# Binding the next pair's operands behind the current pair's adds on VectorE and ScalarE, in the last stage of an attention, token-mixing and MLP kernel

## The chip, the cores and the metric

The kernel runs on one core of a Trainium2 chip. The metric is device time in microseconds, the median of the runs shown. A second number, the span of one profiled execution, is what the rows of the trace add up to.

## The reference, cut to what matters

```
kv  = einsum('bhsd,bhse->bhde', k, v);  out = einsum('bhsd,bhde->bhse', q, kv)
x   = out / sqrt(mean(out*out) + 1e-6) * g_norm          # 8 batches of 576 tokens, 512 features
x   = x + y + relu((x + y) @ w_ch)                       # y: token mixing of x*cos, x*sin
u   = x + transpose(relu(xT @ w_tok1) @ w_tok2)
out = u + relu(u @ w_ch1) @ w_ch2                        # 512 -> 1536 -> 512: the last stage
```

The change touches only the last line, the feed-forward block over the 4608 tokens of u.

## The kernel before

All matrix products are done in float16 pairs: a value is split into a high part and a low part (the rest), and each product is three matmuls on TensorE, high by high, high weight by low operand, and low weight by high operand, summed in PSUM (lines 82 to 84, function `mm3`).

The last stage works on pairs of token blocks of 288 columns. There are 8 pairs, 0 to 7. A pair's two halves of features and two blocks of tokens make a 2 by 2 matrix of blocks, and the product with the weights is done with seven block products in place of eight (products 1 to 7, the Winograd form of Strassen's scheme). So each pair needs seven operands, sums and differences of its four blocks.

`chunks(i)` makes the operands of pair i. It is a generator that is advanced in four steps. The first loads the blocks into the tile `c` (u in the code) by four DMAs from the scratch tensor `u2d` and allocates the operand tiles; the other three compute the operands: ScalarE writes the high parts `o0` (seven of them, index 0 to 6), VectorE writes differences into `t` (four of them) and the low parts `o1`, and at the end ScalarE scales `c` in place. The tiles `o0` and `o1` have one buffer each, so they can be written only when the pair before has read its operands for the last time. In the trace both are called `o`, numbers being left out; in listings of the order, `o40` and `o41` are the high and low operands of pair 4.

`mlp(i)` works off pair i. The hidden features come in six groups g of 128. Each group takes seven products of 6 matmuls with the first weights `wa` into the PSUM tiles `pa`, `pb` and `pc` (products 1, 6, 7 and 4 add up in `pa` one after the other, with a read by ScalarE after each; product 2 goes to `pb`, 5 and 3 to `pc`). ScalarE copies the partial sums to `m`, `u` and `own`; VectorE adds `pb` and `pc` to `own`, forms `pre` from the last of `pc`, and four values `sum`. Of these seven hidden operands ScalarE writes the high parts `gh` (three from `own`, four from `sum`) and VectorE the low parts `gl`. For the second weights `wb`, the tiles `na` (m = 0, 1), `nb` and `nc` take products over all six groups, 18 matmuls each: first product 1 into `na` and product 2 into `nb`, which VectorE adds to `c` (function `add`), then products 5, 6, 7, 3 and 4 into `nc` and `na`, each behind an add that has read what lay in that tile. 504 matmuls make a pair.

Names in the order: `na30` is the tile na of pair 3 for m = 0, `gh35` the high hidden operands of pair 3, group 5. "Body" is used below for the groups' work of a pair, "tail" for the second half of products 5, 6, 7, 3 and 4, "head" for the start of the next body.

What sets the order: the program is written in the order above, and a scheduler then orders each engine's instructions by its own estimate of when they are ready, within the dependences and the program's priorities. The generator's steps are called at fixed places in `mlp`: the first after the adds of products 1 and 2, the next two after the adds of product 6 for m = 0 and m = 1, the last after product 3 of m = 0. The scheduler moves them from there. Each engine runs its queue strictly in that order.

Of the kernel before, what the change touches and what calls it, by code (L numbers as in the profile page):

```python
# [13 lines left out]
AF = mybir.ActivationFunctionType  # L14
ALU = mybir.AluOpType
# [5 lines left out]
SW = 32.0  # L21
# [7 lines left out]
def attn_mixer_kernel(  # L29
# [4 lines left out]
    nc = tc.nc  # L34
# [27 lines left out]
    def bank(name):  # L62
        return ps.tile([P, 512], F32, tag="ps", name=name)
# [88 lines left out]
    def words(w):  # L152
        return (w, 1) if w.dtype == F32 else (w.bitcast(I32), 2)
# [91 lines left out]
    def load_heads(b):  # L245
        o = Batch()
        o.b, o.zh = b, None
        o.kv = []
        for r in range(3 if b else NR + 1):
            load_kv(o, r)  # L250
        o.q = fp.tile([P, HP, SM + P], F32, tag="q", name=f"q{b}", bufs=1)
        qs = qT[b].rearrange("h p s -> p h s")
        nc.sync.dma_start(o.q[:, :, :S], qs)

        nc.sync.dma_start(o.q[:, :, S:], qs[:, :, SM:])
        return o
# [247 lines left out]
    def chunks(i):  # L504

        u = (cp[0] if i % 2 else cw).tile([P, KD, 2, NC], F32, tag="c", name=f"c{i}")
        oh, ol = (cw.tile([P, 7, DH, NC], F16, tag=f"o{j}", name=f"o{i}{j}") for j in range(2))
        if i:
            t = cp[0].tile([P, 4, DH, NC], F32, tag="t", name=f"t{i}")
        else:  # L510

            t = zp.tile([P, KM + 1, DM], F16, tag="zh", name="t0").rearrange("p k d -> p (k d)").bitcast(F32)
            t = t[:, :4 * DH * NC].rearrange("p (x k n) -> p x k n", x=4, k=DH)
        for k in (slice(0, DH), slice(DH, KD)):
            for n in range(2):
                at = (2 * i + n) * NC
                nc.sync.dma_start(u[:, k, n, :], u2d[:, k, at:at + NC])
        b11, b12, b21, b22 = u[:, :DH, 0], u[:, :DH, 1], u[:, DH:, 0], u[:, DH:, 1]
        yield u, oh, ol
        for x, src in ((0, b11), (1, b21), (2, b22)):  # L520
            nc.scalar.activation(oh[:, x], src, AF.Copy, scale=1.0 / SW)
        nc.vector.tensor_tensor(t[:, 0], b12, b11, ALU.subtract)
        nc.vector.tensor_tensor(t[:, 1], b22, t[:, 0], ALU.subtract)
        for x, src in ((0, b11), (1, b21)):
            nc.vector.scalar_tensor_tensor(ol[:, x], src, 1.0 / SW, oh[:, x], ALU.mult, ALU.subtract)
        nc.scalar.activation(oh[:, 3:5], t[:, :2], AF.Copy, scale=1.0 / SW)
        yield
        nc.vector.tensor_tensor(t[:, 2], b12, b22, ALU.subtract)
        nc.vector.tensor_tensor(t[:, 3], b21, t[:, 1], ALU.subtract)
        nc.vector.scalar_tensor_tensor(ol[:, 3:5], t[:, :2], 1.0 / SW, oh[:, 3:5], ALU.mult, ALU.subtract)  # L530
        nc.scalar.activation(oh[:, 5:], t[:, 2:], AF.Copy, scale=1.0 / SW)
        yield
        nc.vector.scalar_tensor_tensor(ol[:, 2], b22, 1.0 / SW, oh[:, 2], ALU.mult, ALU.subtract)
        nc.vector.scalar_tensor_tensor(ol[:, 5:], t[:, 2:], 1.0 / SW, oh[:, 5:], ALU.mult, ALU.subtract)
        nc.scalar.activation(u, u, AF.Copy, scale=1.0 / SW)

    def mlp(i, ck, following):

        u, oh, ol = ck
# [6 lines left out]
        def wide(p, g, acc, first):  # L546
            ws, xs = PRODUCTS[p]
            mm3(acc, [(wa[0][:, g, k, ws], wa[1][:, g, k, ws], oh[:, xs, k], ol[:, xs, k]) for k in range(DH)], first, skip_group_check=True)

        def part(name, g):  # L550
            return cp[0].tile([P, NC], F32, tag=name, name=f"{name}{i}{g}", bufs=2)

        def sums_high(h, g):
            nc.scalar.activation(h.hi[:, 3:], h.s, AF.Copy)  # L554
            nc.vector.tensor_tensor(h.lo[:, 3:], h.s, h.hi[:, 3:], ALU.subtract)  # L555


        def step(n, between=lambda: None):
            g = hidden[n] if n < KH else None
            h = hidden[n - 1] if n else None  # L560
            if g:
                g.a = bank(f"pa{i}{n}")[:, :NC]
                wide(1, n, g.a, True)
                m1 = part("m1", n)
                nc.scalar.activation(m1, g.a, AF.Copy)
            if h:
                wide(7, n - 1, h.a, False)
                u3 = part("u3", n - 1)
                nc.scalar.activation(u3, h.a, AF.Copy)
            if n > 1:  # L570
                sums_high(hidden[n - 2], n - 2)
            between()
            if g:
                pb = bank(f"pb{i}{n}")[:, :NC]
                wide(2, n, pb, True)
                g.own = cp[0].tile([P, 3, NC], F32, tag="own", name=f"own{i}{n}", bufs=2)
                nc.vector.tensor_tensor(g.own[:, 0], pb, m1, ALU.add)
            if h:
                h.c = bank(f"pc{i}{n - 1}")[:, :NC]
                wide(5, n - 1, h.c, True)  # L580
                nc.vector.tensor_tensor(h.own[:, 2], h.c, u3, ALU.add)
            between()
            if g:
                wide(6, n, g.a, False)
                g.u2 = part("u2", n)
                nc.scalar.activation(g.u2, g.a, AF.Copy)
            if h:
                wide(4, n - 1, h.a, False)
                nc.scalar.activation(h.own[:, 1], h.a, AF.Relu)
                nc.scalar.activation(h.own[:, 0::2], h.own[:, 0::2], AF.Relu)  # L590
                between()
                wide(3, n - 1, h.c, False)
                h.hi = cp[0].tile([P, 7, NC], F16, tag="gh", name=f"gh{i}{n - 1}", bufs=KH)
                h.lo = cp[0].tile([P, 7, NC], F16, tag="gl", name=f"gl{i}{n - 1}", bufs=KH)
                nc.scalar.activation(h.hi[:, :3], h.own, AF.Copy)
                pre = part("pre", n - 1)
                nc.vector.tensor_tensor(pre, h.c, h.u2, ALU.add)  # L597
                h.s = cp[0].tile([P, 4, NC], F32, tag="sum", name=f"sum{i}{n - 1}", bufs=2)
                nc.vector.scalar_tensor_tensor(h.s[:, 0], pre, 0.0, h.own[:, 0], ALU.max, ALU.subtract)
                nc.vector.scalar_tensor_tensor(h.s[:, 2], pre, 0.0, h.own[:, 2], ALU.max, ALU.subtract)  # L600
                nc.vector.tensor_tensor(h.s[:, 1], h.own[:, 2], h.s[:, 0], ALU.subtract)
                nc.vector.tensor_tensor(h.s[:, 3], h.own[:, 1], h.s[:, 1], ALU.subtract)
                nc.vector.tensor_tensor(h.lo[:, :3], h.own, h.hi[:, :3], ALU.subtract)  # L603

        def narrow(p, m, g, acc, first):
            ws, xs = PRODUCTS[p]
            h = hidden[g]
            part = (wb[0][:, g, m, ws], wb[1][:, g, m, ws], h.hi[:, xs], h.lo[:, xs])
            mm3(acc, [part], first=first and g == 0, last=g == KH - 1, skip_group_check=True)

        def add(acc, m, half, n, last=False):
            ct = half * MH + m
            dst = u[:, ct, n, :]
            nc.vector.scalar_tensor_tensor(dst, acc, 1.0 / SW**2, dst, ALU.mult, ALU.add)  # L614
            if last:
                at = (2 * i + n) * NC
                nc.sync.dma_start(outf[:, ct, at:at + NC], dst)
# [7 lines left out]
        def side(g):  # L625
            for acc, p, name in ((pa, 1, "na"), (pb, 2, "nb")):
                for m in range(MH):
                    if g == 0:
                        acc[m] = bank(f"{name}{i}{m}")[:, :NC]
                    narrow(p, m, g, acc[m], True)  # L630

        step(KH, lambda: side(next(start)))
        for g in start:
            side(g)
# [3 lines left out]
        for m in range(MH):  # L638
            add(pa[m], m, 0, 0)
            add(pb[m], m, 0, 0, True)  # L640
        nxt = next(following, None)

        def run(p, m, acc, first):
            if acc[m] is None:
                acc[m] = bank(f"nc{i}{m}")[:, :NC]
            for g in range(KH):
                narrow(p, m, g, acc[m], first)
# [67 lines left out]
    nxt = load_heads(1)  # L715
# [40 lines left out]
    for b in range(B):  # L756
        loaded.clear()
        if b == 0:
# [10 lines left out]
            src, _ = words(w_tok1)  # L769
# [49 lines left out]
        o, nxt = nxt, after  # L819
# [10 lines left out]
    for i in range(pairs):  # L830
        ck = mlp(i, ck, chunks(i + 1) if i + 1 < pairs else iter(()))
# [40 lines left out]
```

## Time and profile before

| | us |
|---|---|
| median of 3 runs | 1155.57 |
| lowest, highest | 1155.48, 1162.52 |
| the profiled execution's own time | 1159.02 |
| its span | 1157.3 |
| TensorE busy in the span | 1086.3 |
| VectorE, ScalarE busy | 825.4, 560.2 |

The time is that of the whole execution, the span what the profiler records of it; 1.7 us of the profiled execution lie outside its span. The last stage, from the first pair on, begins near 640 us. One thing to know for reading the timelines: a matmul's row shows how long it was under way, while the next one starts some 0.12 us behind it.

### The profile page before, as it was taken

Reading aid. Unit: us, or ns where it says so; the run is one execution under the profiler, and the core shown is the slowest. Engines: PE = TensorE matmul, PEld = TensorE weight load, DVE = VectorE, ACT = ScalarE, POOL = GpSimd, SP = SyncE. Lnnn points to the kernel's source line nnn. Section 1 sums busy time; section 2 is a strip of 40 time slices with the busy share of each in tenths; the row PEclk is TensorE's granted clock in tenths of the full one; section 3 lists DMA queues with packets and bytes.
Section 4 is the critical chain, followed back from the end, with each engine's and each line's share of the span. In section 5 each row is a group of like instructions: output and inputs, shape, how many; then the busy total and the mean of one; then the engine's idle time right before and its main releaser. Section 6 shows DMA issues by size and latency. Waiting matters only on the chain.

```text
span 1157.3 us, 21691 instructions
## 1 busy us (share of the span) xinstructions
PE 1086.3 (94%) x8884; PEld 821.8 (71%) x8884; DVE 825.4 (71%) x1475; ACT 560.2 (48%) x958; POOL 225.7 (20%) x290
## 2 busy tenths in 40 slices
PE   4779988998998999989999999999999999999998
PEld 3566766675875767657677777777777777777776
DVE  4998858777787887868746494848577584848483
ACT  3757526455455454554623373625355362726260
POOL 2351033462642725426100000000000000000000
PEclk9779989998998999989999999999999999999999
DMA  9535564775748738663192801011010202010101
GB/s 323 194 131 103 118 168 112 200 181 130 237 95 209 190 98 216 148 159 90 44 273 56 300 1 57 26 42 42 27 57 12 72 12 73 1 66 18 37 7 42
DMA packets 146084, 126.36 MB, mean 109 GB/s; under 512 B 93184, under 2 KB 121984, under 8 KB 145984
## 3 DMA queue, kind: packets, MB, share of 16 engines
q1 hardware_dynamic: 140608, 104.53, 33.9%
q0 software_dynamic: 5376, 20.45, 5.1%
q8 instruction: 69, 1.13, 0.4%
q14 instruction: 31, 0.25, 0.1%
HBM read 74.29 MB, written 29.88 MB: 90 GB/s over the span
## 4 chain that ended last, share of the span: by engine, by line
PE 37%; DVE 30%; DMA 13%; ACT 9%; POOL 6%; issue 4%; SPq 1%; POOLq 0%; ACTq 0%; DVEq 0%
DMA xt<-xs 3%; PE na L82 3%; PE na L84 3%; PE na L83 3%; DVE gl L555 3%; DVE gl L603 3%; DVE cs L358 3%; DMA c<-u2d 2%; DMA u2d<-R 2%; PE pa L82 2%; ACT gh L554 2%; PE pa L83 2%; PE pa L84 2%; PE nc L84 1%; PE nc L82 1%
## 5 line engine op out<-in xcount | busy, mean ns | idle before, releaser
L82 PE MATMUL py<-wmh,zh 128*128 128x256 f16 (+1 forms) x576 | 165.9, 288 | 4.3 <-ACT zh L361 2.7
L83 PE MATMUL py<-wml,zh 128*128 128x256 f16 (+1 forms) x576 | 165.8, 288 | 0.0
L84 PE MATMUL py<-wmh,zl 128*128 128x320 f16 (+1 forms) x512 | 146.0, 287 | 3.2 <-DVE zl L363 3.2
L82 PE MATMUL na<-gh,wbh 128*128 128x288 f16 x384 | 107.6, 286 | 9.3 <-DVE c L614 9.3
L82 PE MATMUL pa<-o,wah 128*128 128x288 f16 x384 | 108.6, 286 | 1.1 <-DVE pre L597 1.1
L83 PE MATMUL pa<-o,wah 128*128 128x288 f16 x384 | 109.3, 286 | 0.0
L83 PE MATMUL na<-gl,wbh 128*128 128x288 f16 x384 | 109.3, 286 | 0.0
L84 PE MATMUL na<-gh,wbl 128*128 128x288 f16 x384 | 109.2, 286 | 0.0
L84 PE MATMUL pa<-o,wal 128*128 128x288 f16 x384 | 108.6, 286 | 0.0
L82 PE MATMUL pr<-uh,wch 128*128 128x256 f16 (+1 forms) x256 | 77.1, 302 | 11.0 <-ACT uh L419 11.0
L83 PEld LDWEIGHTS <-wbh 128*128 128x128 f16 x672 | 65.7, 98 | 26.8 <-issue 10.4
L555 DVE TENSOR_TENSOR gl<-sum,gh 128x1152 f16<-128x1152 f32 x48 | 65.0, 1354 | 24.3 <-ACT gh L554 23.5
L83 PE MATMUL pr<-ul,wch 128*128 128x256 f16 (+1 forms) x256 | 77.3, 302 | 5.1 <-DVE ul L422 5.1
L83 PEld LDWEIGHTS <-wah 128*128 128x128 f16 x672 | 65.7, 98 | 18.5 <-issue 2.0
L82 PEld LDWEIGHTS <-wah 128*128 128x128 f16 x672 | 65.7, 98 | 16.6
L84 PEld LDWEIGHTS <-wbl 128*128 128x128 f16 x672 | 65.7, 98 | 16.6
L82 PEld LDWEIGHTS <-wbh 128*128 128x128 f16 x672 | 65.7, 98 | 16.6
L84 PEld LDWEIGHTS <-wal 128*128 128x128 f16 x672 | 65.7, 98 | 16.6
L84 PE MATMUL pr<-uh,wcl 128*128 128x256 f16 (+1 forms) x256 | 77.1, 301 | 0.0
L614 DVE SCALAR_TENSOR_TENSOR c<-na,c 128x288 f32<-128x288 f32 x64 | 28.9, 452 | 64.5 <-PE na L84 64.5
L82 PEld LDWEIGHTS <-zh 128*128 128x128 f16 x576 | 56.9, 99 | 21.1 <-ACT zh L361 3.4
L301 POOL TENSOR_TENSOR ri<-ss,mhalf 128x8 f32<-128x8 f32 x40 | 70.2, 1756 | 2.4
(292 smaller groups left out, 2931.4 us busy)
## 6 DMA issues: line engine op xcount, KB each, us to landing
q<-in_q SPq DMA_DIRECT2D x8, 1152.0 KB, 7.1
c<-u2d SPq DMA_DIRECT2D x32, 288.0 KB, 4.3
out<-c SPq DMA_DIRECT2D x64, 144.0 KB, 1.7
k<-in_k SPq DMA_DIRECT2D x24, 256.0 KB, 6.6
v<-in_v SPq DMA_DIRECT2D x24, 256.0 KB, 6.7
wa_r<-in_w_ch SPq DMA_DIRECT2D x24, 256.0 KB, 4.2
wb_r<-in_w_ch SPq DMA_DIRECT2D x24, 256.0 KB, 4.3
wad<-wa POOLq DMA_DIRECT2D x24, 224.0 KB, 3.4
```

The costliest lines, as they stand in the source:

```text
L82: nc.tensor.matmul(acc, ah, bh, start=first and i == 0, stop=False, **more)
L83: nc.tensor.matmul(acc, ah, bl, start=False, stop=False, **more)
L84: nc.tensor.matmul(acc, al, bh, start=False, stop=last and i == n - 1, **more)
L301: nc.gpsimd.tensor_tensor(ri, ss, mhalf, ALU.pow)
L358: nc.vector.tensor_tensor(cs, cs, x.unsqueeze(1).to_broadcast([P, 2, DM]), ALU.mult)
L554: nc.scalar.activation(h.hi[:, 3:], h.s, AF.Copy)
L555: nc.vector.tensor_tensor(h.lo[:, 3:], h.s, h.hi[:, 3:], ALU.subtract)
L603: nc.vector.tensor_tensor(h.lo[:, :3], h.own, h.hi[:, :3], ALU.subtract)
L614: nc.vector.scalar_tensor_tensor(dst, acc, 1.0 / SW**2, dst, ALU.mult, ALU.add)
```

## The change

`keep_in_program_order` puts an edge from an instruction to the one that was written just ahead of it on the same engine: it may not be queued earlier than that one. It makes no instruction wait for another's end. `placed` applies it, for all pairs but the first, to six instructions of the generator: the first high part, the first difference of each of the two difference steps, the high parts 5 and 6, the low part 2 and the scaling of `c`. Instructions between them aren't bound. The generator's first step, with the loads, is now written ahead of the last body step, so that its edges refer to the places where the later steps are called.

```
+        def placed(ins):
+            if i:
+                tc.keep_in_program_order(ins)
         yield u, oh, ol
         for x, src in ((0, b11), (1, b21), (2, b22)):
-            nc.scalar.activation(oh[:, x], src, AF.Copy, scale=1.0 / SW)
-        nc.vector.tensor_tensor(t[:, 0], b12, b11, ALU.subtract)
+            ins = nc.scalar.activation(oh[:, x], src, AF.Copy, scale=1.0 / SW)
+            if x == 0:
+                placed(ins)
+        placed(nc.vector.tensor_tensor(t[:, 0], b12, b11, ALU.subtract))
         nc.vector.tensor_tensor(t[:, 1], b22, t[:, 0], ALU.subtract)
...
-        nc.vector.tensor_tensor(t[:, 2], b12, b22, ALU.subtract)
+        placed(nc.vector.tensor_tensor(t[:, 2], b12, b22, ALU.subtract))
...
-        nc.scalar.activation(oh[:, 5:], t[:, 2:], AF.Copy, scale=1.0 / SW)
-        yield
-        nc.vector.scalar_tensor_tensor(ol[:, 2], b22, 1.0 / SW, oh[:, 2], ALU.mult, ALU.subtract)
+        placed(nc.scalar.activation(oh[:, 5:], t[:, 2:], AF.Copy, scale=1.0 / SW))
+        yield
+        placed(nc.vector.scalar_tensor_tensor(ol[:, 2], b22, 1.0 / SW, oh[:, 2], ALU.mult, ALU.subtract))
         nc.vector.scalar_tensor_tensor(ol[:, 5:], t[:, 2:], 1.0 / SW, oh[:, 5:], ALU.mult, ALU.subtract)
-        nc.scalar.activation(u, u, AF.Copy, scale=1.0 / SW)
+        placed(nc.scalar.activation(u, u, AF.Copy, scale=1.0 / SW))
...
+        nxt = next(following, None)
         step(KH, lambda: side(next(start)))
...
-        nxt = next(following, None)
-
         def run(p, m, acc, first):
```

Up to the last stage no engine's order changes. In it, three places matter.

VectorE, the end of pair 3's body, from the last `pre` to the add of product 1 (line numbers after are 7 higher). Before:

```order
L597 TENSOR_TENSOR pre35_10000<-pc35_9951,u235_9898 128x288
L525 SCALAR_TENSOR_TENSOR o41_10054<-c4_10052,o40_10053 128x576 x2
L599 SCALAR_TENSOR_TENSOR sum35_10002<-pre35_10000,own35_9882 128x288
L600 SCALAR_TENSOR_TENSOR sum35_10002<-pre35_10000,own35_9882 128x288
L533 SCALAR_TENSOR_TENSOR o41_10054<-c4_10052,o40_10053 128x576
L530 SCALAR_TENSOR_TENSOR o41_10054<-t4_10055,o40_10053 128x1152
L601 TENSOR_TENSOR sum35_10002<-own35_9882,sum35_10002 128x288
L614 SCALAR_TENSOR_TENSOR c3_9335<-na30_9935,c3_9335 128x288
```

and now:

```order
L604 TENSOR_TENSOR pre35_10008<-pc35_9959,u235_9898 128x288
L532 SCALAR_TENSOR_TENSOR o41_9927<-c4_9925,o40_9926 128x576
L606 SCALAR_TENSOR_TENSOR sum35_10010<-pre35_10008,own35_9882 128x288
L607 SCALAR_TENSOR_TENSOR sum35_10010<-pre35_10008,own35_9882 128x288
L608 TENSOR_TENSOR sum35_10010<-own35_9882,sum35_10010 128x288
L621 SCALAR_TENSOR_TENSOR c3_9208<-na30_9943,c3_9208 128x288
```

Of the next pair's low parts one (index 1) still stands ahead of the add of `na30`; one more of that size, the low part 2 and the double low part 3 and 4 now stand behind it.

TensorE, the same place: the last matmuls ahead of product 6 into `na30` (the first of which ends each piece). Before, ahead of it stand products 1 and 2 of pair 4's first group (`pa40`, `pb40`):

```order
L83 MATMUL pb40_10282<-o41_10054,wah_6749 128x288
L84 LDWEIGHTS wal_6750
L84 MATMUL pb40_10282<-o40_10053,wal_6750 128x288
L82 LDWEIGHTS wbh_7391
L82 MATMUL na30_9935<-gh30_9638,wbh_7391 128x288
```

and now the last ones of product 2 of pair 3:

```order
L83 MATMUL nb31_9955<-gl35_10006,wbh_7391 128x288
L84 LDWEIGHTS wbl_7392
L84 MATMUL nb31_9955<-gh35_10005,wbl_7392 128x288
L82 LDWEIGHTS wbh_7391
L82 MATMUL na30_9943<-gh30_9638,wbh_7391 128x288
```

Of pair 4's first two groups 52 matmuls were queued within pair 3's tail before; now it is 24, and all of them behind the first matmuls of product 6.

VectorE, the differences `t`. Before, those for pair 5 stood in the body of pair 4:

```order
L577 TENSOR_TENSOR own42_10392<-pb42_10385,m142_10373 128x288
L522 TENSOR_TENSOR t5_10772<-c5_10769 128x576
L555 TENSOR_TENSOR gl40_10356<-sum40_10360,gh40_10355 128x1152
L523 TENSOR_TENSOR t5_10772<-c5_10769,t5_10772 128x576
L528 TENSOR_TENSOR t5_10772<-c5_10769 128x576
L529 TENSOR_TENSOR t5_10772<-c5_10769,t5_10772 128x576
```

and now those for pair 4 stand among the adds of pair 3's tail:

```order
L562 TENSOR_TENSOR gl35_10006<-sum35_10010,gh35_10005 128x1152
L532 SCALAR_TENSOR_TENSOR o41_9927<-c4_9925,o40_9926 128x576
L621 SCALAR_TENSOR_TENSOR c3_9208<-nc30_10060,c3_9208 128x288
L621 SCALAR_TENSOR_TENSOR c3_9208<-na30_9943,c3_9208 128x288
L529 TENSOR_TENSOR t4_9928<-c4_9925 128x576
L621 SCALAR_TENSOR_TENSOR c3_9208<-nc31_10107,c3_9208 128x288
L621 SCALAR_TENSOR_TENSOR c3_9208<-na31_9947,c3_9208 128x288
L535 TENSOR_TENSOR t4_9928<-c4_9925 128x576
L530 TENSOR_TENSOR t4_9928<-c4_9925,t4_9928 128x576
```

The four differences have left the body. The double low parts (indices 3 and 4, then 5 and 6) and low part 2 follow them in the tail, and on ScalarE the high parts 3 to 6 and the scaling of `c`. The DMA queue's order is the same before and after.

## Rows read from the trace of the kernel before

**Rows 1.** The page: busy time, and the granted clock in 40 slices.
```profile
PE 1086.3 (94%) x8884; PEld 821.8 (71%) x8884; DVE 825.4 (71%) x1475; ACT 560.2 (48%) x958; POOL 225.7 (20%) x290
...
PEclk9779989998998999989999999999999999999999
```

**Rows 2.** Busy time by stretches of the last stage, one stretch a pair.
```profile
core 0: us, PE busy (x) PEld busy (x) DVE busy (x) ACT busy (x) POOL busy (x), PEclk, DMA share, GB/s
...
883.80:947.70 63.90, 61.95 (x504) 49.29 (x504) 43.17 (x79) 30.23 (x49) 0.00 (x0) 1.00 0.12 38
...
sum 466.70, PE 452.73 PEld 359.98 DVE 306.87 ACT 210.25 POOL 0.00; mean PE 64.68 PEld 51.43 DVE 43.84 ACT 30.04 POOL 0.00
```

**Rows 3.** Who TensorE waited for, 640 us to the end: total, times, longest.
```profile
PE na L82 <- DVE c L614: 9.3, 6, 1.9
PE pa L82 <- DVE pre L597: 1.1, 2, 0.9
```

**Rows 4.** Timeline of TensorE, pair 3's end: start, length, operation, idle before.
```profile
872.35 0.29 PE L84 MATMUL pa<-o,wal 128*128 128x288 f16 x1
...
881.66 0.29 PE L84 MATMUL pb<-o,wal 128*128 128x288 f16 x1
883.88 0.28 PE L82 MATMUL na<-gh,wbh 128*128 128x288 f16 x1 [1.94 <-DVE c L614]
...
907.28 0.29 PE L84 MATMUL pa<-o,wal 128*128 128x288 f16 x1
```

**Rows 5.** Timeline of VectorE, the same stretch.
```profile
876.39 1.36 DVE L555 TENSOR_TENSOR gl<-sum,gh 128x1152 f16<-128x1152 f32 x1 [1.74 <-ACT gh L554]
877.67 1.05 DVE L603 TENSOR_TENSOR gl<-own,gh 128x864 f16<-128x864 f32 x1
878.64 0.45 DVE L597 TENSOR_TENSOR pre<-pc,u 128x288 f32<-128x288 f32 x1
879.00 1.41 DVE L525 SCALAR_TENSOR_TENSOR o<-c,o 128x576 f16<-128x576 f32 x2
880.34 0.45 DVE L599 SCALAR_TENSOR_TENSOR sum<-pre,own 128x288 f32<-128x288 f32 x1
880.71 0.45 DVE L600 SCALAR_TENSOR_TENSOR sum<-pre,own 128x288 f32<-128x288 f32 x1
881.08 0.75 DVE L533 SCALAR_TENSOR_TENSOR o<-c,o 128x576 f16<-128x576 f32 x1
881.75 1.35 DVE L530 SCALAR_TENSOR_TENSOR o<-t,o 128x1152 f16<-128x1152 f32 x1
883.01 0.45 DVE L601 TENSOR_TENSOR sum<-own,sum 128x288 f32<-128x288 f32 x1
883.38 0.45 DVE L614 SCALAR_TENSOR_TENSOR c<-na,c 128x288 f32<-128x288 f32 x1
```

**Rows 6.** Timeline of ScalarE, the same stretch.
```profile
874.33 0.68 ACT L590 ACTIVATE own<-own 128x576 f32<-128x576 f32 x1 [3.10 <-DVE own L581]
874.91 0.39 ACT L589 ACTIVATE own<-pa 128x288 f32<-128x288 f32 x1
875.21 1.15 ACT L554 ACTIVATE gh<-sum 128x1152 f16<-128x1152 f32 x1
...
907.60 0.41 ACT L589 ACTIVATE own<-pa 128x288 f32<-128x288 f32 x1 [13.12 <-PE pa L84]
```

**Rows 7.** Timeline of VectorE in the body of pair 4.
```profile
913.47 0.76 DVE L522 TENSOR_TENSOR t<-c 128x576 f32<-128x576 f32 x1 [1.19 <-DMA c<-u2d]
...
916.46 0.76 DVE L523 TENSOR_TENSOR t<-c,t 128x576 f32<-128x576 f32 x1 [0.96 <-DMA c<-u2d]
...
923.08 1.36 DVE L555 TENSOR_TENSOR gl<-sum,gh 128x1152 f16<-128x1152 f32 x1 [0.74 <-ACT gh L554]
...
928.96 1.36 DVE L555 TENSOR_TENSOR gl<-sum,gh 128x1152 f16<-128x1152 f32 x1 [0.74 <-ACT gh L554]
```

**Rows 8.** Busy time in the rest of pair 3's tail, columns as in rows 2.
```profile
883.90:907.50 23.60, 23.60 (x193) 18.86 (x193) 9.10 (x19) 3.65 (x8) 0.00 (x0) 1.00 0.13 44
```

## The prediction

> **What bounds the kernel now.** The page comes first: TensorE is busy for 94% of the span, VectorE for 71%, and from the middle of the span on the granted clock is at its full level, 2.4 GHz [rows 1]. So in the last stage time can only be won where TensorE stands still. The table by stretches tells how much that is: over seven stretches from 690.6 us on TensorE is busy for 452.73 of 466.70 us, and a pair's 504 matmuls take 61.95 us, 0.1229 us each [rows 2]; I count 0.1225 where they run without a gap. Some of the missing 14 us lie behind the last matmul and can't be touched. What can be touched stands in the list of waits: 9.3 us in six stops of the first matmul of product 6 into `na`, which waits for an add on VectorE (L614), and 1.1 us in two stops at `pa` [rows 3]. That is 10.4 us, the ceiling of any gain here and 0.9% of the time. There are seven places where one pair passes into the next; the first had no such stop.
>
> The timelines then show how a stop arises, at the end of pair 3. TensorE issues the last matmul of `pb` at 881.66 and the next one, into `na`, at 883.88, after 1.94 us of idling [rows 4]. The add that it waits for starts at 883.38 on VectorE, which has been working without a break since 876.39: two `gl`, a `pre`, and then, between the `sum` of the last group, four steps for the next pair's low parts, L525 twice, L533 and L530 [rows 5]. The chain of ScalarE that starts it begins late, too. The last matmul of the last group's product 4 is issued at 872.35 [rows 4]. ScalarE can read such a result 0.32 us after that matmul's start: 907.28 and 907.60 in a place where it was waiting for it [rows 4, 6]. But here it reads at 874.91, since the step ahead of it (L590) waited for VectorE until 874.33 [rows 6]. It is late by 874.91 - 872.35 - 0.32 = 2.24 us. I call this VectorE's backlog, B.
>
> **The change, part by part.** *The low parts that leave the chain.* One L525 (0.67 us by the step from 881.08 to 881.75 of the like L533), L533 (0.67) and L530 (881.75 to 883.01, 1.26) no longer stand ahead of the add: 2.60 us less [rows 5]. One low part stays there (0.67). The chain from ScalarE's read of product 4 to TensorE's go is now, by starts: read to `gh` 0.30, `gh` to `gl` 1.18 [rows 5, 6], `gl` L555 1.28, `gl` L603 0.97, `pre` 0.36, one low part 0.67, three `sum` 0.37 each, and 0.50 from the add's start to the matmul [rows 4, 5]. The sum is 6.37 us, where it was 883.88 - 874.91 = 8.97. After pairs 0, 2, 4 and 6 a fourth `sum` stands ahead of the add as well, at most 0.45 more.
>
> *The matmuls that leave the cover.* Before, 76 matmuls lay between the end of product 4 and product 6 of `na`; now, with pair 4's first products moved behind, it is 53 after the pairs 1, 3 and 5, 56 after 2, 4 and 6, and 57 after pair 0 (counted in the order). TensorE's own work is the same, so this costs nothing by itself, but it arrives at the add earlier: after 6.49 us in place of 9.31, or after 6.86 and 6.98. The cover loses 2.82 us where the chain loses 2.60. So what is to be won does not hang on the low parts but on B. With 0.20 us from the end of product 4's issue to the read (0.32 less a matmul's 0.12), the stop is 0.20 + B + 6.37 - 6.49 = 0.08 + B after an odd pair, and at most 0.20 + B + 6.82 - 6.86 = 0.16 + B after an even one.
>
> *The backlog.* The trace does not show B in the new order, so I bound it. Its upper end is today's 2.24. Its lower end is zero, and a reckoning of VectorE's body work leads there. From one `gl` L555 to the next in the crowded part of the body it is 5.88 us, of which 0.74 waiting for `gh`: 5.14 us of work for a group [rows 7]. In the new order VectorE has to do, between the first `pre` of the body and the fourth `sum` of group 4, five groups' work less one `gl` (1.28) and less two `own` adds (0.4 each): 25.7 - 2.1 = 23.6 us, and with two waits of 0.74 us 25.1. The first `pre` can begin when product 3 of group 0 is through, 72 matmuls into the body, at 8.8 + 0.2 = 9.0 us; the fourth `sum` then ends at 34.1. Product 4 of group 5 ends 279 matmuls into the body after an odd pair, 274 after an even one, at 34.2 or 33.6; ScalarE has read it 0.5 us later, at 34.7 or 34.1. So the sum is there when ScalarE comes to it, and B is between 0 and 0.3. What has left the body to make this so: four differences `t` of some 0.67 us each and two waits for the load of `c`, 1.19 and 0.96 us [rows 7], together 4.8 us. What has come into it is group 0's work, which before began in the tail ahead. I take a stop of 0.2 us at each of the seven places, nearer to the lower end, since the reckoning ends there: 1.4 us.
>
> One thing in this sum is a matter of how rows are read. A VectorE step of 0.45 us is followed by the next one 0.37 us after its start [rows 5], so I count starts, not lengths. The Trainium skill ("VectorE: DVE Perf Modes", "The DRAIN you can't avoid") says that the next operation does not start until the pipeline is empty; counted by full lengths the chain would be 0.57 us longer, and seven times that would put the time at an estimated 1150.6. The row shows an overlap of 0.08 us at every one of these steps, and the sum goes by it.
>
> *The two stops at `pa`* (1.1 us) wait for a `pre`, and so for the same backlog; I count them as gone.
>
> *What moved into the tail.* VectorE is busy for 9.10 of 23.60 us there, ScalarE for 3.65 [rows 8]. Four differences, two double and two single low parts (2.7 + 2.5 + 1.3 = 6.5 us) and on ScalarE some 5 us of high parts and scaling fit in. TensorE's work hides them, and the nearest due time is that of the second L532, low part 0: it stands behind four adds, a `sum`, `gh` (1.18) and `gl` (1.28) and is done 4.4 us after the add of `na30` starts, while TensorE needs it 54 matmuls after it starts product 6, at 0.5 + 6.6 = 7.1 us. The cover is 2.7 us. All later operands have more, being due at the next body's first matmuls or after. The early call of the generator's first step moves no load: the DMA queue's order is unchanged.
>
> Sum: 10.4 - 1.4 = 9.0 us won. The profiled execution took 1159.02 us (1157.3 of span and 1.7 outside) and would take 1150.0; that execution was 3.45 us above the median of the runs, and I carry the difference over to the median: 1155.57 - 9.0 = 1146.6 us.
>
> **The rivals.** *Some backlog stays.* The reckoning of B takes VectorE as running without other waits, and 25 us of it leave room for an error of a microsecond. At B = 1 the stops are 1.1 us each, 7.7 in all; the gain is 2.7 and the time 1152.9. For it: the new order has VectorE idle at the head of the body and crowded behind, as now. Against it: the 4.8 us that left the body.
>
> *The backlog stays as it is, and the kernel gets slower.* This is one mechanism at one place: the cover of product 6 shrinks by 2.82 us while the chain shrinks by 2.60. At B = 2.24 each of the seven stops is 2.3 us, 16.2 together in place of 10.4, and the time is 1161.4. It decides from B = 1.4 on, where seven stops of 1.48 us make today's 10.4. For it speaks that today's B of 2.24 comes from the same engine doing the same work; against it, that the reckoning would have to be wrong by 1.4 us at every pair.
>
> *The next pair's operands come late.* If the second L532 is done over 2.7 us later than I work out, TensorE stops there, and from 4.2 us on (2.7 and the 1.5 won at a place) the change loses. Nothing in the tail's rows is near that full [rows 8].
>
> *The change does not do what it says* is ruled out for the adds, which the order shows ahead of three of the four low parts; that one low part stays ahead is in the sum.
>
> **How the numbers follow.** The time is 1155.57 - 10.4 + 7 x stop. I give 0.70 to a backlog under about 0.45 us (1145.2 to 1149), with 1146.6 for its likeliest value; 0.17 to a backlog from there to 1.4 (1149 to 1155.6); 0.08 to more (1161.4 at 2.24); 0.03 to late operands; 0.02 to anything else. The range for 8 in 10 goes from just under the ceiling, 1144.8, to 1153.0, which takes in the first case and most of the second. A change of 1%, 11.6 us, is about what a measurement of this kernel can tell from none. Faster by more than that would take more than all of TensorE's idle time here: 0.04. Slower by more than that needs a backlog over 3.1 us or operands late by some 6 us: 0.04. The rest, 0.92, is within 1%.
>
> **What would show it.** In the new profile the list of waits for TensorE should have `na` on the add at under 0.4 us a time, and the `pa` stops should be gone; a pair should take 61.9 to 62.2 us from product 6 to product 6 in place of 63 to 65. ScalarE's L596 (now L589) should start within 0.6 us of product 4's end, and VectorE should show the `t` and low parts in the tail. The prediction is wrong if that ScalarE step is still 1 us or more late (then the stop is that long), or if TensorE shows stops at `pa` or `pb` behind a low part `o`.

## The result and the profile after

The changed kernel takes 1146.62 us (median of 6 runs, 1144.02 to 1148.35) where the kernel before took 1156.62 (6 runs, 1155.48 to 1162.52) beside it: a ratio of 0.990, 95% interval 0.988 to 0.993. The profiled execution of the changed kernel took 1148.35 us, 1146.6 of it span.

The page of the kernel after, busy time and granted clock, answers to [rows 1]:

```profile
PE 1079.8 (94%) x8884; PEld 819.2 (71%) x8884; DVE 823.6 (72%) x1475; ACT 561.9 (49%) x958; POOL 229.4 (20%) x290
...
PEclk9889998999999999989999999999999999999999
```

TensorE's share looks unchanged, since busy time and span both went down; its busy time fell in the stages ahead of the last one (590.6 us before, 584.8 after) and hardly within it (495.7 and 495.0). The last stage by itself tells more. From the first matmul into `pa` to the end of the span it took 1157.3 - 647.6 = 509.7 us before and 1146.6 - 648.0 = 498.6 after, 11.1 us less; up to it the two profiled executions are within 0.4 us.

Busy time by stretches, one from product 6 to the next product 6, columns as in [rows 2]:

```profile
877.15:939.10 61.95, 61.90 (x505) 49.31 (x504) 43.46 (x79) 31.11 (x49) 0.00 (x0) 1.00 0.12 39
815.32:877.15 61.83, 61.83 (x505) 49.31 (x504) 42.71 (x77) 30.26 (x48) 0.00 (x0) 1.00 0.12 39
```

A pair now takes hardly longer than its matmuls, whose 504 spacings of 0.1225 us make 61.7 us: 61.8 to 62.0 us from product 6 to product 6, where it was 62.8 to 65.1. The list of TensorE's waits from 640 us on, which had eight stops [rows 3], is empty; in the groups by line 0.2 us are left, at the first matmul of product 6:

```profile
L82 PE MATMUL na<-gh,wbh 128*128 128x288 f16 x384 | 106.0, 286 | 0.2
```

The end of pair 3 on TensorE, then on ScalarE, then on VectorE, answers to [rows 4 to 6] (lines 7 higher):

```profile
870.44 0.29 PE L84 MATMUL pa<-o,wal 128*128 128x288 f16 x1
...
876.94 0.29 PE L84 MATMUL nb<-gh,wbl 128*128 128x288 f16 x1
877.15 0.28 PE L82 MATMUL na<-gh,wbh 128*128 128x288 f16 x1
```

```profile
870.77 0.41 ACT L596 ACTIVATE own<-pa 128x288 f32<-128x288 f32 x1
871.07 1.16 ACT L561 ACTIVATE gh<-sum 128x1152 f16<-128x1152 f32 x1
```

```profile
872.26 1.36 DVE L562 TENSOR_TENSOR gl<-sum,gh 128x1152 f16<-128x1152 f32 x1 [1.44 <-ACT gh L561]
873.54 1.05 DVE L610 TENSOR_TENSOR gl<-own,gh 128x864 f16<-128x864 f32 x1
874.50 0.45 DVE L604 TENSOR_TENSOR pre<-pc,u 128x288 f32<-128x288 f32 x1
874.87 0.75 DVE L532 SCALAR_TENSOR_TENSOR o<-c,o 128x576 f16<-128x576 f32 x1
875.54 0.45 DVE L606 SCALAR_TENSOR_TENSOR sum<-pre,own 128x288 f32<-128x288 f32 x1
...
876.64 0.82 DVE L621 SCALAR_TENSOR_TENSOR c<-na,c 128x288 f32<-128x288 f32 x2
...
880.33 0.75 DVE L532 SCALAR_TENSOR_TENSOR o<-c,o 128x576 f16<-128x576 f32 x1
...
883.96 0.75 DVE L529 TENSOR_TENSOR t<-c 128x576 f32<-128x576 f32 x1
```

ScalarE's read of product 4 (L596) starts 0.33 us after the last matmul of that product: B is 0.01, where it was 2.24. That 2.24 was not the same at every pair: before the change B was 0.0 after pair 0, which had no stop, and 0.8, 1.8, 2.2, 2.2, 2.2 and 1.2 after pairs 1 to 6, while the chain of these six stayed at 8.97 us, so their stops, 1.1 to 2.1 us long, followed B. Now it is 0.13 after pair 0 and 0.01 after the others. From that read to product 6 it is 877.15 - 870.77 = 6.38 us, and product 6 starts 0.21 us after the matmul ahead of it, 0.09 more than a matmul's spacing. The other low parts and the `t` stand behind the add, in the tail.

The list of VectorE's waits shows what left the body. From 690 to 1144 us the kernel before had

```profile
DVE t L522 <- DMA c<-u2d: 13.2, 6, 4.1
...
DVE t L523 <- DMA c<-u2d: 2.2, 2, 1.2
```

that is 15.4 us in six pairs in which VectorE stood at a `t`, with the body's steps queued behind it, until the load of `c` had landed. After the change there is no such wait.

### The profile page after: what moved, and what is told of

It is laid out like the page before. It is cut to its first block, busy times and chain, and to the rows that moved or that the text cites. A ratio compares the mean times of both kernels' runs of the same rounds, so it can differ in the third digit from the quotient of the medians.

```text
span 1146.6 us, 21657 instructions
## 1 busy us (share of the span) xinstructions
PE 1079.8 (94%) x8884; PEld 819.2 (71%) x8884; DVE 823.6 (72%) x1475; ACT 561.9 (49%) x958; POOL 229.4 (20%) x290
## 4 chain that ended last, share of the span: by engine, by line
PE 54%; DVE 18%; DMA 9%; ACT 8%; POOL 7%; issue 4%; SPq 1%; POOLq 0%; ACTq 0%; DVEq 0%
PE na L82 4%; PE pa L84 4%; PE pa L83 4%; PE pa L82 4%; PE na L84 4%; PE na L83 4%; DVE cs L358 2%; DMA xt<-xs 2%; PE pc L84 2%; PE pc L83 2%; PE pc L82 2%; PE nc L82 2%; PE nc L84 2%; PE nc L83 2%; DMA u2d<-R 2%
## 5 line engine op out<-in xcount | busy, mean ns | idle before, releaser
L82 PEld LDWEIGHTS <-zh 128*128 128x128 f16 x576 | 57.0, 99 | 23.4 <-DMA zh<-zt 4.1
L83 PEld LDWEIGHTS <-zh 128*128 128x128 f16 x576 | 57.0, 99 | 15.9
```

What stands on the lines that cost most here:

```text
L82: nc.tensor.matmul(acc, ah, bh, start=first and i == 0, stop=False, **more)
L83: nc.tensor.matmul(acc, ah, bl, start=False, stop=False, **more)
```

## The experiments

The theories, in short. **A** is the prediction's sum: a stop at product 6 is 0.20 us + B + chain - cover, and what is won hangs on B. **T**: what made B is the four differences `t` and their wait for the load in VectorE's body. **L**: what gains is that low parts stand behind the add. The other rivals are named where they come up. The times of the experiments are medians of 4 to 10 runs, put against the kernel before run on the same chip (1156.66 us median for t_only, no_t, l2u_only and body8, 1156.76 for the other four). All but t_pool keep the early call of the generator's first step. Because the stages ahead of the last one vary by several us from one execution to another, the table also has the last stage of the profiled execution alone, from its first `pa` matmul to the end of the span.

| kernel | median, us | ratio, 95% interval | last stage, us |
|---|---|---|---|
| before | 1156.62 | | 509.7 |
| changed | 1146.62 | 0.988 to 0.993 | 498.6 |
| t_only | 1146.28 | 0.989 to 0.992 | 498.8 |
| no_t | 1169.01 | 1.006 to 1.013 | 517.7 |
| no_t_again | 1168.12 | 1.006 to 1.011 | 518.7 |
| l2u_only | 1146.55 | 0.989 to 0.993 | 499.5 |
| h0_only | 1169.13 | 1.007 to 1.013 | 521.2 |
| t_pool | 1162.70 | 1.002 to 1.006 | 513.5 |
| body8 | 1146.25 | 0.989 to 0.992 | 498.3 |
| body16 | 1167.62 | 1.006 to 1.013 | 520.7 |

**t_only.** Of the six placed instructions only the first of each two `t` keeps its place.

```
-            if x == 0:
-                placed(ins)
...
-        placed(nc.scalar.activation(oh[:, 5:], t[:, 2:], AF.Copy, scale=1.0 / SW))
+        nc.scalar.activation(oh[:, 5:], t[:, 2:], AF.Copy, scale=1.0 / SW)
...   (low part 2 and the scaling of c likewise)
```

> Only the two differences t are bound; the high and low parts and the scaling are free. Three single low parts (2.0 us) then stand ahead of the add of product 1, where it is one in the changed kernel and 3.27 us of them before; the cover of product 6 is 68 matmuls, 8.33 us; no t is left in the body. Theory A (a stop lasts 0.20 + B + chain - cover, with B VectorE's backlog, which is 0 to 0.3 once the t are out of the body): the chain is 6.37 + 1.34 - 0.37 = 7.34 us, the stop 0.2 + 0.3 + 7.34 - 8.33 < 0, so TensorE has no stops and the time is that of the changed kernel, 1146 to 1148 us. Rival L (what costs is the low parts ahead of the add, as the change's words say): the stops follow their length, half the gain is lost, 1151 us. Rival T (only the differences in the body cost): 1146.6 us.

The time is that of the whole change. After pairs 1 to 6 B is 0.0 and the chain 7.34 to 7.35 us, with more low parts ahead of the add than in the changed kernel; the cover is 68 matmuls (8.33 us), and TensorE does not stop at `na`. Two of the six placed instructions, with the early call, are enough; the half gain that L expected is wrong.

**no_t and no_t_again.** All placed but the two `t`.

```
-        placed(nc.vector.tensor_tensor(t[:, 0], b12, b11, ALU.subtract))
+        nc.vector.tensor_tensor(t[:, 0], b12, b11, ALU.subtract)
...
-        placed(nc.vector.tensor_tensor(t[:, 2], b12, b22, ALU.subtract))
+        nc.vector.tensor_tensor(t[:, 2], b12, b22, ALU.subtract)
```

> All is bound but the two differences t, which return to the body. One single and two double low parts (3.2 us) stand ahead of the add after pairs 1 to 6, about as much as before the change (3.27); the cover falls to 63 matmuls, 7.72 us. Theory A: the chain is 6.37 - 0.37 + 0.37 + 2 x 1.26 = 8.89 us, the stop 0.20 + B + 8.89 - 7.72 = 1.37 + B, with B at 2.24 or more (the t wait for the load at the head of the body), so 3.6 us or more at six places: at least 22 us of stops in place of 10.4, 1168 us or more, slower than before. Rival L: as many low parts ahead as before, so 1156 us. Rival T: the t are in the body as before, so 1156 us.

The kernel is slower than before, on the side that A said. Who TensorE waited for in it, from 640 us on (total, times, longest):

```profile
PE na L82 <- DVE c L621: 14.5, 6, 2.7
PE nc L82 <- ACT gh L561: 1.7, 1, 1.7
PE pa L82 <- DVE own L584: 0.3, 1, 0.3
```

The chain is 8.89 to 8.90 us, the cover 63 matmuls (7.72), and B between 0.88 and 1.44, so A had B too high here; the stops are 2.3 to 2.8 us all the same. VectorE waits for the load at the `t` for 34.6 + 6.0 us. This is the prediction's second rival, made real in part: cover taken away while some of the backlog stays. A's sizes did not come: where it expected at least 22 us of stops at `na`, the spacing of the matmuls shows 15.5. The rest of the 19.1 us by which the last stage is longer than the changed kernel's lies mostly in the stops at `nc` and `pa` and in a lower clock, shown below. That the median met A's 1168 is therefore no proof of its sum.

Its first profiled execution took 1161.8 us and the others 1168 to 1170, so it was run again.

> The kernel with all but the two differences placed, once more, to see whether its time is that of its first profiled execution (1161.8, seven stops of 2.4 to 2.9 us) or that of its other executions (1168 to 1170). If the stops alone make the time, theory A's sum gives 1162 to 1163. If it is 1168 to 1170 again in the profiled execution, the trace must show 6 to 8 us elsewhere: a granted clock below 1.00 in the last stage after the stops, or stops at another place.

It was 1169.11 in the profiled execution. 6.2 of the 7.3 us by which the spans differ lie ahead of the last stage (its first `pa` matmul is at 648.59 in place of 642.37), at neither of the places that the expectation named; and the stops are six in either execution, not seven. The last stage is 1.1 us longer, and both executions have something that the list of waits does not show. The stretches around the stop at 887.62 in the second one (the column behind POOL is the granted clock):

```profile
885.00:887.50 2.50, 0.52 (x5) 0.28 (x3) 2.50 (x5) 0.00 (x0) 0.00 (x0) 1.00 0.00 0
...
888.60:889.60 1.00, 1.00 (x6) 0.64 (x5) 0.50 (x3) 1.00 (x2) 0.00 (x0) 0.50 0.00 1
...
891.60:892.60 1.00, 1.00 (x11) 0.79 (x9) 0.00 (x0) 0.00 (x0) 0.00 (x0) 1.00 0.00 0
```

TensorE stands still for 2.3 us, goes on at 2.4 GHz for three matmuls and then gets 1.2 GHz until about 891.3, with its matmuls 0.24 us apart:

```profile
887.62 0.28 PE L82 MATMUL na<-gh,wbh 128*128 128x288 f16 x1 [2.10 <-DVE c L621]
...
888.06 0.45 PE L82 MATMUL na<-gh,wbh 128*128 128x288 f16 x1
888.30 0.45 PE L83 MATMUL na<-gl,wbh 128*128 128x288 f16 x1
```

Some 14 matmuls at 0.12 us more are 1.7 us on top of the stop. It came behind two of the six stops there, behind one of six in the first execution, and behind none of the six in the kernel before (2.1 us and less, clock 1.00 throughout).

**l2u_only.** Only low part 2 and the scaling of `c` are placed; the `t` stand in the body, as before.

```
-            if x == 0:
-                placed(ins)
-        placed(nc.vector.tensor_tensor(t[:, 0], b12, b11, ALU.subtract))
+        nc.vector.tensor_tensor(t[:, 0], b12, b11, ALU.subtract)
...   (t[:, 2] and the high parts 5 and 6 likewise)
```

> Only the last step is bound, low part 2 on VectorE and the scaling of c on ScalarE; the t stay in the body. Two single low parts (1.34 us) stand ahead of the add, and some 49 matmuls of the next pair are still queued in the tail, so the cover is 77 to 83 matmuls, 79 (9.68 us) after most pairs. Theory A: the chain is 6.37 + 0.67 - 0.37 = 6.67 us, the backlog stays near 2.24, the stop is 0.20 + 2.24 + 6.67 - 9.68 < 0: no stops, 1146 to 1148 us, with the backlog still there in ScalarE's read of product 4 (about 2 us late). Rival T: the t are in the body, so the stops stay, 1156 us. Rival L: 1.34 us of low parts ahead in place of 3.27, so three quarters of the gain, 1149 us.

The time is again that of the whole change, with a single stop, of 1.2 us of idle time after pair 2. But A's detail is wrong: ScalarE's read of product 4 is not late (B 0.0); the chain behind it is, at 7.6 to 9.1 us and once 11.6. ScalarE's order has changed. The read (L594) now stands ahead of the step that waits for VectorE (L595), where it stood behind it; here after pair 4:

```profile
929.87 0.41 ACT L594 ACTIVATE own<-pa 128x288 f32<-128x288 f32 x1 [0.72 <-PE pa L84]
931.60 0.68 ACT L595 ACTIVATE own<-own 128x576 f32<-128x576 f32 x1 [1.32 <-DVE own L586]
```

So B alone does not tell that VectorE is on time. After pairs 3 to 5 backlog and chain together were 11.2 us before and are 8.4 to 9.1 here, a fall of 2.1 to 2.8 us; the low parts and the one `sum` that no longer stand ahead of the add make 2.3. The cover, 76 matmuls before, is 79 (0.4 us more) after those pairs. So the stops can be had away with the `t` in the body, by taking low parts out of the chain while the cover is kept, and T as the only way is wrong.

**h0_only.** One placed instruction, the first high part on ScalarE, with the early call of the generator's first step.

```
-        placed(nc.vector.tensor_tensor(t[:, 0], b12, b11, ALU.subtract))
+        nc.vector.tensor_tensor(t[:, 0], b12, b11, ALU.subtract)
...   (the other four likewise; the high part 0 stays placed)
```

> One of the six placed instructions alone: the first high part on ScalarE, with the early call of the generator's first step. The differences t stay in the body ahead. After even pairs two single low parts stand ahead of the add, after odd pairs two double ones as well, while the cover is 63 or 64 matmuls throughout (7.7 to 7.8 us). Theory A with B of about 1.2 us as the run with all but the two t placed had it: even pairs chain 6.67, stop 0.2 + 1.2 + 6.67 - 7.8 = 0.2 us; odd pairs chain about 9.5, stop 0.2 + 1.2 + 9.5 - 7.7 = 3.2 us; three odd and four even places make some 10.5 us over the changed kernel's 1146.3, so about 1157, the time of before. The stops should alternate, in step with the low parts. Rival L (low parts behind the add are what gains, by their count): half of the change's gain, about 1151. Rival 'B alone decides': the same stop after every pair.

The stops at `na` alternate as A said, measured by the spacing of the matmuls: 3.3 to 3.5 us after odd pairs, 0.8 after pair 0 and 0.5 after the other even ones. The terms are not A's: after odd pairs B is 1.3 to 1.4 and the chain 9.56, but after even ones B is 0.0 and the chain about 8.0, where A had 1.2 and 6.67. The time is 12 us longer than A's, mostly because of stops that no theory had named. The list of TensorE's waits:

```profile
PE na L82 <- DVE c L621: 11.3, 7, 3.3
PE nc L82 <- ACT gh L561: 6.9, 4, 1.7
```

The four at `nc` make 7.5 us with the 0.16 us each that a matmul's row hides; by the spacing those at `na` make 12.5, and behind the stop after pair 1 the granted clock was 0.50, 1.2 GHz, from 759.4 to 762.8 (1.7 us). Together that is most of the 22.6 us by which the last stage is longer than the changed kernel's. After an even pair the two double low parts stand behind the add, ahead of the last `sum`, and product 5 into `nc` waits for the `gh` made from it. On VectorE, then TensorE, after pair 4:

```profile
952.62 0.45 DVE L621 SCALAR_TENSOR_TENSOR c<-na,c 128x288 f32<-128x288 f32 x1
952.99 1.35 DVE L537 SCALAR_TENSOR_TENSOR o<-t,o 128x1152 f16<-128x1152 f32 x1
...
954.99 1.35 DVE L541 SCALAR_TENSOR_TENSOR o<-t,o 128x1152 f16<-128x1152 f32 x1
...
956.99 0.45 DVE L609 TENSOR_TENSOR sum<-own,sum 128x288 f32<-128x288 f32 x1
```

```profile
958.68 0.28 PE L82 MATMUL nc<-gh,wbh 128*128 128x288 f16 x1 [1.72 <-ACT gh L561]
```

Moving work behind the first add only helps if the next thing due, here that `sum`, does not stand behind it. In the changed kernel it stands ahead of them.

**t_pool.** The kernel before, with the differences of each next pair made by GpSimd.

```
-        nc.vector.tensor_tensor(t[:, 0], b12, b11, ALU.subtract)
+        (nc.gpsimd if i else nc.vector).tensor_tensor(t[:, 0], b12, b11, ALU.subtract)
...   (t[:, 1] to t[:, 3] likewise)
```

> The kernel before, no instruction placed, but the four differences t of each next pair computed by GpSimd in place of VectorE. The matmuls queued ahead of product 6 stay as many as before (46 to 52 of the next pair; cover 77 to 94, mostly 85) and two or three low parts still stand ahead of the add. Theory T (what made B is the four differences and their wait for the load in VectorE's body): B about 0 to 0.3, chain about 7.3 where one pair of single low parts is ahead of the add, no stop of TensorE, time 1146 to 1148. Rival (B comes from the order of the body's own steps, whatever t does): B stays at about 2.2; with the longer cover that alone would give stops of 0.20 + 2.2 + 7.3 - 10.4, none, so the time does not tell the two apart, but ScalarE's read of product 4 does. A third case: GpSimd's steps slow VectorE's down, which would show as longer rows of VectorE beside them and a B over 0.5.

The third case came. After pairs 3 to 6, B is 0.0 to 0.01 and TensorE does not stop at `na`, as T says. After the first pairs it is not so clean: B is 0.14, 0.0 and 2.99 after pairs 0, 1 and 2, with stops of 0.9, 0.1 and 1.4 us. And TensorE stops within the body, 6.2 us in five stops at `pc` and 3.3 in one at `pa`. The timeline of GpSimd, and that of VectorE beside it:

```profile
854.73 1.41 POOL L522 TENSOR_TENSOR t<-c 128x576 f32<-128x576 f32 x1 [58.59 <-DMA c<-u2d]
856.23 2.09 POOL L523 TENSOR_TENSOR t<-c,t 128x576 f32<-128x576 f32 x1
858.28 1.62 POOL L528 TENSOR_TENSOR t<-c 128x576 f32<-128x576 f32 x1
859.86 1.61 POOL L529 TENSOR_TENSOR t<-c,t 128x576 f32<-128x576 f32 x1
```

```profile
856.98 1.66 DVE L599 SCALAR_TENSOR_TENSOR sum<-pre,own 128x288 f32<-128x288 f32 x1
858.56 1.66 DVE L600 SCALAR_TENSOR_TENSOR sum<-pre,own 128x288 f32<-128x288 f32 x1
860.14 1.65 DVE L601 TENSOR_TENSOR sum<-own,sum 128x288 f32<-128x288 f32 x1
861.71 0.44 DVE L581 TENSOR_TENSOR own<-pc,u 128x288 f32<-128x288 f32 x1
```

While GpSimd works, VectorE's `sum` takes 1.66 us in place of 0.45: one step of the one for each step of the other, 3.6 us more for the three, where four `t` on VectorE take 2.7. The step that TensorE needs next, L581 at 861.71, stands behind them, and TensorE stops for 1.56 us.

The Trainium skill ("SBUF — State Buffer", "SBUF: two separate sides") says that GpSimd and a VectorE step with two inputs from SBUF can't hold the ports that they share at the same time, and that the later one waits for the whole of the other; the rows agree.

The granted clock fell once here, too: behind the stop at `pa`, 3.33 us of idle time up to 667.40, it was 0.50.

```profile
667.10:670.40 3.30, 3.00 (x13) 1.87 (x13) 3.27 (x7) 2.98 (x6) 0.00 (x0) 0.50 0.00 0
```

**body8 and body16.** The changed kernel with 8 or 16 additions of 128x288 on VectorE that nothing reads, 0.37 us each, in every pair's body.

```
+                if n == KH - 2:
+                    for _ in range(8):
+                        junk = part("junk", n)
+                        tc.keep_in_program_order(nc.vector.tensor_tensor(junk, h.own[:, 0], h.own[:, 2], ALU.add))
```

> The changed kernel with eight idle adds of 128x288 on VectorE (0.37 us each, 2.96 us; their result is not used) put into the work of group 3 of each pair. Nothing else is added, and the cover becomes 50 matmuls (6.13 us) after pairs 1 to 6, 66 after pair 0. Theory A: some 0.75 to 1.3 us of it falls into VectorE's waits, B rises to between 1.4 and 2.1, the chain (one sum fewer) is 6.0, the stop 0.07 + B: 1.5 to 2.2 us at six places, 9 to 13 us, 1155.5 to 1160 us. A rival by which VectorE, busy for 72% of the span, has room for 3 us a pair: 1146.6 us, no stops.

With eight the time does not move: B is 0.0, the chain 6.00, the spacing at product 6 0.20 us after pairs 1 to 6. A's forecast of 1155.5 to 1160 was wrong in B, and the rival by which VectorE has room came true. Its waits gave way. From 690 to 1144 us, the changed kernel, then the one with eight:

```profile
DVE gl L562 <- ACT gh L561: 20.6, 21, 1.6
```

```profile
DVE gl L562 <- ACT gh L561: 9.1, 8, 1.2
```

These are 11.5 of the 20.7 us that the additions make in seven pairs; the waits at the adds of the tail (L621, now L625) fell from 67.0 to 55.8 us.

> The changed kernel with 16 idle adds of 128x288 on VectorE in each pair's body, ahead of the sums of group 3 (extra work that nothing reads; twice that of the run with eight). At 0.37 us from one step to the next they are 5.92 us. The run with eight kept its lag at 0.0 because VectorE's own waits gave way; in its trace about 0.34 us of such waiting was left at the last sum, so the second eight (2.96 us) should come through as B of about 2.6 us. Theory A (the stop at product 6 is 0.20 us + B + chain - cover; VectorE's backlog makes B): chain 6.00, cover 50 matmuls = 6.13, stop 2.6 to 2.7 us at each of six or seven places, some 16 to 18 us, time about 1163. Rival (VectorE has so much room that its work in the body does not matter, and the old stops came from the early-queued matmuls or the place of the low parts alone): B stays under 0.5 and the time is 1146 to 1148.

With sixteen the loss comes: B is 3.38 after pairs 1 to 6 (6.30 after pair 0), more than the 2.6 expected, the chain 5.33, shorter by as much, and the cover 50 matmuls (6.13 us). A's sum gives 0.20 + 3.38 + 5.33 - 6.13 = 2.78 us a place; TensorE's matmuls show two stops there of 1.91 and 0.88, together 2.79. The list of TensorE's waits:

```profile
PE nc L82 <- DVE own L584: 14.6, 8, 2.3
PE na L82 <- DVE c L625: 5.8, 8, 1.4
```

The larger part of the loss has moved to a matmul ahead of product 6, which waits for L584, the add of `pb` in the same pair's last group, and that stands behind the extra work (`junk`). After pair 3, on VectorE and TensorE:

```profile
879.62 0.82 DVE L609 TENSOR_TENSOR junk<-own 128x288 f32<-128x288 f32 x2
880.36 0.45 DVE L584 TENSOR_TENSOR own<-pb,m 128x288 f32<-128x288 f32 x1
```

```profile
880.86 0.28 PE L82 MATMUL nc<-gh,wbh 128*128 128x288 f16 x1 [1.75 <-DVE own L584]
```

The last stage is 22.1 us longer than the changed kernel's. So VectorE's body had room for some 3 us of work a pair, and not for 6.

## Why the prediction was right, point by point

- *What bounds the kernel.* Right: the change touches no engine's work, and the 11.1 us of the last stage are TensorE's stops (counted under *The sum*).
- *The ceiling.* Mis-sized. 10.4 us was the idle time in the list of waits. The spacing of the matmuls gives more: the stop at 883.88 is 883.88 - 881.66 - 0.12 = 2.10 us against 1.94 of idle [rows 4], since a matmul's row of 0.29 us covers 0.16 of it. Over eight stops this makes 11.7 us; two more of 0.24 us, at the `pc` right behind the two at `pa`, show no idle time at all, so what could be won was 12.2.
- *The chain.* 6.37 and 6.82 at most predicted, 6.37 to 6.38 and 6.86 to 6.88 measured. Counting starts was right; by full lengths it would have been 0.57 us longer, and no run shows that. The passage of the Trainium skill that the prediction reads in this way ("VectorE: DVE Perf Modes", "The DRAIN you can't avoid") itself adds that a next operation which is not held starts earlier.
- *The cover.* 53, 56 and 57 matmuls, so the stop is 0.08 + B and 0.16 + B; measured 0.09 after odd pairs and 0.21 to 0.22 after even ones.
- *The backlog.* Predicted between 0 and 0.3, measured 0.01 at six places and 0.13 at the first. The step that decides the sign was right. Its margin says too little: by that reckoning the fourth `sum` is ready 0.6 us ahead of ScalarE at the end of pair 3, and in the trace it is 0.25, yet 2.96 us of extra work in body8 did no harm, since VectorE's waits gave way.
- *The sum.* Seven stops were to cost 1.4 us and cost 3 x 0.09 + 4 x 0.21 = 1.1. With the 12.2 of before the gain is 11.1 us in place of 9.0, which is what the last stage shows; the medians show 10.0. That the predicted 1146.6 met the measured 1146.62 so closely is luck: the prediction had the gain too small and stood on a median of before of 1155.57, and the runs beside the changed kernel had 1156.62.
- *"What is to be won does not hang on the low parts but on B"* holds for this order (t_only, no_t, body16), but not for every one: l2u_only loses the stops with the `t` in the body, by a shorter chain under a long cover.
- *Operands late in the tail.* Not seen: the second L532 is through at 881.1, 3.9 us after product 6 started, where it was due 6.6 us after.
- *The two stops at `pa`* are gone, as counted.

Which part of the `t` in the body made B, their four steps (2.7 us) or the wait for the load (2.6 us a pair), was not tried by itself, since an earlier load would need another buffer of `c`. That 2.96 us of work alone did nothing in body8 speaks for the wait, but body8 has another order, and the length of the wait does not order B: after pairs 1 to 6 of the kernel before, waits of 4.1, 1.8, 3.5, 2.2, 2.7 and 1.2 us in the body go with B of 0.8, 1.8, 2.2, 2.2, 2.2 and 1.2, and no_t, with some 7 us of such waits a pair, has less B. This stays open.

## What to carry to other kernels

Where TensorE waits at the seam between two blocks, write the stop as the sum of read, backlog, chain and cover, all counted by starts, and ask which term the change moves: an edit that takes 2.6 us off the chain and 2.8 off the cover is nothing by itself. Look in an in-order queue for steps of the next block that wait for a load while steps of this block stand behind them; bind those first (here two bindings of six gained all of it, and the other four without them lost 1%, though two of those four by themselves, in l2u_only, gained all of it in another way). Judge a stage by its own length in the trace where the stages ahead of it vary by more than the effect.

## What the runs showed of the hardware that was not expected

- TensorE's granted clock can fall behind a stop: in the two executions of no_t three stops of 2.3 to 2.7 us were followed by some 3 us at 1.2 GHz, which cost about 1.7 us each, while nine others of 2.3 to 2.8 us were not; the same came behind one of h0_only's three stops of 3.3 to 3.5 us and behind t_pool's one of 3.5 us. What tells them apart stays open.
- GpSimd's differences made VectorE's `sum` take 1.66 us in place of 0.45; four steps of GpSimd cost VectorE more than the 2.7 us that they took off it.
- Idle time before a matmul at 2.4 GHz was 0.16 us less than the stop wherever both were read, by the overlap of the row ahead of it.
